# 32-column matmul tiles, and batch 2's softmax sums by way of DRAM, in a fused attention and feed-forward kernel

## The chip, the cores and the metric

The kernel runs on one core of one Trainium2 chip. The metric is the device time of one execution in microseconds. Eleven runs of the kernel before on one chip lie within 0.2 % (506.83 to 507.83 us). All comparisons here are between runs in the fast state of the chip. The rounds ran on several chips, on which the kernel before took 507.07 to 507.42 us in the median; so differences between runs of different rounds are good to some 0.3 us, and the ratios to the kernel before are the safer measure.

## The reference

Eight batches of eight heads go through an attention whose keys and values are first projected from 1024 positions to 64; its result goes through a feed-forward layer.

```python
k_proj = einsum('ks,bhsd->bhkd', E, k)          # q, k, v: 8 x 8 x 1024 x 64; E, F: 64 x 1024
v_proj = einsum('ks,bhsd->bhkd', F, v)
scores = q @ k_proj.transpose(0, 1, 3, 2) / 8
attn = exp(scores - max); attn = attn / (sum(attn) + 1e-9)
x = (attn @ v_proj), heads side by side         # 8192 x 512
h = x @ w_in                                    # 512 x 2048
g = h * clip(h + 3, 0, 6) / 6
out = g @ w_out                                 # 2048 x 512
```

## The kernel before

TensorE (PE) works nearly all the time (busy 99 % of the span), mostly on the feed-forward layer. Between groups of its matmuls the kernel makes short *visits* to the attention of later batches. One batch takes about 60 us: 2 blocks of 512 tokens, each with 16 groups of `w_in` (4 matmul rounds each) and 4 groups of `w_out` (16 rounds each). So a batch has 8 *stages* of four `w_in` groups and one `w_out` group, and a visit is hung on a stage.

Every stationary operand of 128 columns is split in two, so that two matmuls work side by side on the array (in the chain of waits 256 of them take 27.75 us, 128 rounds of 0.216 us):

```python
    width = [P // 2]
    def in_columns(ps, stationary, moving, **flags):
        for lo in range(0, stationary.shape[-1], width[0]):
            nc.tensor.matmul(ps[lo:lo + width[0]], stationary[:, lo:lo + width[0]], moving, **flags)
```

Projecting a batch frees its raw k and v and starts a chain: the projected keys are transposed by DMA, mostly the queries too, and only when that has landed does GpSimd issue the next batch's loads (for batch 4 it sat idle 35.23 us until the keys had landed, and issued the first load at 139.58 us). The two projections share one bank. The sums of exponentials are found on PE, and from batch 3 on they take a detour: logarithm and exponential give reciprocals in a few rows, which are stored in DRAM and read back once for each head, spread over 64 partitions.

```python
        def project(self, alloc):
            ps = self.ps = alloc()
            for so in range(SO):
                for e in range(2):
                    in_columns(ps[e * KP:(e + 1) * KP], ef_t[e][:, so, :], kqv[self.b]["kv"[e]][:, :, so, :],
                               start=(so == 0), stop=(so == SO - 1))
        def turn(self):
            nc.sync.dma_start_transpose(self.kT, self.kp.rearrange("p h a d -> p (h a d)"))
            last = self.kT[:1, 0, :1]
            if self.b not in (2, 3):
                qT_dma[self.b] = q_transposed(self.b)
                last = qT_dma[self.b][:1, 0, 0, :1]
            if self.b + 1 < B:
                mark = att.tile([1, 1], bf16, tag="mark", name="mark")
                nc.gpsimd.tensor_copy(mark, last)
                load_kqv(self.b + 1, "kvq" if self.b in (1, 3) else "qkv")
        # ...
        def all_sums(self, alloc):                 # batches 3 to 7: 32-column tiles, two banks
            tiles = [alloc() for _ in range(2)]
            for h in range(H):
                j, a, c = h // 2, h % 2, h % 4
                nc.tensor.matmul(tiles[h // 4][32 * c:32 * c + 32].rearrange("p (r n) -> p r n", r=2),
                                 halves.rearrange("p t i -> p (t i)"), self.aT[j][:, :, a, :],
                                 start=True, stop=True)
            return tiles
        def spread(self, den):
            few = att.tile([P, 2, TOK], f32, tag="few", name="few", bufs=1)
            inverse(few, den)
            rows = dram.tile([H, NB, TOK], f32, tag="rows", name="rows")
            nc.sync.dma_start(out=rows.rearrange("(k c) t n -> (c t) k n", k=2), in_=few[::16])
            self.recs = [rec_tile() for _ in range(KO)]
            for h in range(H):
                nc.sync.dma_start(out=..., in_=rows[h:h + 1]...to_broadcast([D, NB * TOK]))
```

Here `b` is the batch in the feed-forward layer, `second` is batch b+1 and `third` batch b+2; `n` is the stage. Batch 2 (at b = 1) has four visits of its own with its sums on PE. From b = 3 on the plan is: scores of three of the four pairs of heads, with the projection of the batch after next right behind them, then sums with the first values, products, and the last values.

```python
                if (b, n) == (2, 3):
                    return lambda: third.projected(pmm), nothing
                if n == 0:
                    return nothing, lambda: second.some_scores(
                        (1, 2, 3), ((pmm, pmm), (pat, pat), (pat, pmm)), third)
                if n == 2:
                    return second.sums_and_values, nothing
                if n == 5:
                    return second.first_products, nothing
                if n == 6:
                    return lambda: second.last_values(third), nothing
```

The softmax here doesn't subtract the row's maximum and nothing guards it: scores larger than these inputs give would overflow.

## Time and profile before

| | before |
|---|---|
| time, median of three runs | 507.55 us (507.52 to 507.98) |
| span of the profiled run | 505.5 us |
| PE busy | 498.9 us (99 %), 4858 matmuls |
| VectorE, ScalarE busy | 48 %, 51 % |
| instruction queue | 38 packets, 0.62 MB |

In the page, a line such as `PE 498.9 (99%) x4858` is an engine's busy time, its share of the span and its instructions. In a timeline, a row is a start, a duration, an engine, a source line, the operation and its tiles; at its end, in brackets, stand the idle time of the engine before it and what ended that. The chain of waits is the series of pieces that ended last, back from the end. The idle time in brackets runs from the end that the profile gives the last matmul. Counted from start to start, less one round of 0.216 us, the same wait is some 0.2 us longer; the expectations mostly count so (2.45 us where the brackets have 2.29). What these views say of this kernel is in the prediction.

### The profile page before, as it was taken

To read this page: it belongs to the slowest core of one execution; us is meant where nothing else is said; L and a number is where in the kernel's file an instruction comes from. 1 tells how busy PE (TensorE), PEld (TensorE's weight loads), DVE (VectorE), ACT (ScalarE), POOL (GpSimd) and SP (SyncE) were. 2 spreads that over 40 slices of the span, in tenths; PEclk is the share of its full clock that TensorE was granted. 3 is DMA by queue.
4 is the path that set the end of the run, shared out by engine and by line. 5 is a ranking of instruction groups with operands and counts; after the bars stand their busy time and mean duration, and the time that the engine had idled before them with its cause. 6 is when DMAs were issued, how large, how long until landed. Compare 5 with 4: busy or idle time off the path is not lost.

```text
span 505.5 us, 11242 instructions
## 1 busy us (share of the span) xinstructions
PE 498.9 (99%) x4858; PEld 259.5 (51%) x4858; DVE 245.1 (48%) x384; ACT 256.1 (51%) x438; POOL 38.7 (8%) x58
## 2 busy tenths in 40 slices
PE   8999999999999999999999999999999999999997
PEld 4554554554454555545554555545555555555554
DVE  3572736865733564536635455533752446334420
ACT  3757466566565444653555544654455544344431
POOL 8620020020020020020001000000000000000000
PEclk9999999999999999999999999999999999999999
DMA  9999979799299999699416992248110361101112
GB/s 168 198 205 208 200 131 231 142 155 202 73 151 194 230 169 190 137 154 249 123 43 118 205 249 69 61 100 209 43 43 29 82 164 43 39 26 43 43 43 84
DMA packets 78074, 66.30 MB, mean 131 GB/s; under 512 B 36216, under 2 KB 67192, under 8 KB 78024
## 3 DMA queue, kind: packets, MB, share of 16 engines
q0 software_dynamic: 32480, 29.36, 37.4%
q1 hardware_dynamic: 45320, 35.89, 27.7%
q8 instruction: 38, 0.62, 0.5%
q10 hardware_dynamic: 224, 0.33, 0.2%
q14 instruction: 12, 0.10, 0.1%
HBM read 69.73 MB, written 16.94 MB: 171 GB/s over the span
## 4 chain that ended last, share of the span: by engine, by line
PE 85%; DMA 12%; POOL 2%; ACT 1%; issue 0%; DVE 0%; ACTq 0%; POOLq 0%
PE mm L172 79%; DMA q<-in_q_dram 6%; DMA w_in_sb<-in_moe_w_in_dram 2%; PE at L172 2%; DMA v<-in_v_dram 2%; DMA qT<-q 2%; PE at L251 1%; PE at L233 1%; PE mm L251 1%; POOL q L106 1%; PE mm L271 1%; POOL k L110 1%; ACT aT L242 0%; PE mm L233 0%; POOL v L110 0%
## 5 line engine op out<-in xcount | busy, mean ns | idle before, releaser
L512 DVE SCALAR_TENSOR_TENSOR g<-r,mm 128x512 bf16<-128x512 f32 x256 | 173.5, 686 | 178.7 <-ACT r L511 177.9
L172 PE MATMUL mm<-w_out_sb,g 128*64 128x512 bf16 (+2 forms) x2080 | 235.0, 376 | 0.2 <-DVE g L512 0.2
L172 PE MATMUL mm<-xT,w_in_sb 128*64 128x512 bf16 x2048 | 231.5, 379 | 0.3
L511 ACT ACTIVATE r<-mm 128x512 f32<-128x512 f32 x256 | 152.2, 599 | 74.5 <-PE mm L172 73.5
L172 PEld LDWEIGHTS <-w_in_sb 128*64 128x64 bf16 x2048 | 117.2, 110 | 104.0 <-issue 0.8
L172 PEld LDWEIGHTS <-g 128*64 128x64 bf16 x2080 | 116.2, 110 | 105.5 <-issue 7.0
L546 ACT COPY o_sb<-mm 128x512 f32<-128x512 f32 x55 | 32.2, 586 | 126.7 <-PE mm L172 126.7
L264 DVE TENSOR_TENSOR xT<-at,rec 128x512 bf16<-128x512 f32 x42 | 26.5, 681 | 6.5 <-ACT rec L184 6.5
L242 ACT ACTIVATE aT<-at 128x512 bf16<-128x512 f32 x38 | 20.2, 615 | 9.1 <-PE at L233 9.1
L208 DVE CAST kp<-at 64x512 bf16<-64x512 f32 x12 | 7.7, 677 | 15.9 <-PE at L172 15.9
L223 POOL COPY mark<-qT 1x1 bf16<-1x1 bf16 x4 | 0.7, 176 | 165.0 <-DMA qT<-q 165.0
L242 ACT ACTIVATE aT<-mm 128x512 bf16<-128x512 f32 x18 | 10.3, 613 | 3.9 <-PE mm L233 3.9
L546 DVE COPY o_sb<-mm 128x512 f32<-128x512 f32 x8 | 5.5, 687 | 13.8 <-PE mm L172 13.8
L172 PE MATMUL at<-v,f_t 128*64 128x512 bf16 x48 | 11.4, 381 | 0.3 <-DMA v<-in_v_dram 0.3
L172 PE MATMUL at<-k,e_t 128*64 128x512 bf16 x48 | 11.6, 382 | 0.0
L264 DVE TENSOR_TENSOR xT<-mm,rec 128x512 bf16<-128x512 f32 x14 | 9.0, 685 | 4.3 <-PE mm L251 4.3
L184 ACT ACTIVATE rec<-rec 128x1024 f32<-128x1024 f32 x10 | 10.6, 1060 | 0.3
L178 ACT ACTIVATE rec<-mm 128x512 f32<-128x512 f32 x10 | 5.5, 595 | 7.9 <-PE mm L251 5.4
L178 ACT ACTIVATE few<-mm 128x512 f32<-128x512 f32 x10 | 5.4, 594 | 7.4 <-PE mm L271 7.4
L93 PE MATMUL mm<-ones 128*128 128x512 bf16 x18 | 7.4, 549 | 1.5 <-DVE halves L84 1.5
L172 PEld LDWEIGHTS <-e_t 128*64 128x64 bf16 x56 | 5.7, 110 | 6.0 <-issue 1.8
L211 DVE CAST vp<-at 64x512 bf16<-64x512 f32 x12 | 8.3, 694 | 0.4
(73 smaller groups left out, 155.0 us busy)
## 6 DMA issues: line engine op xcount, KB each, us to landing
out_dram<-o_sb SPq DMA_DIRECT2D x63, 256.0 KB, 3.0
rec<-rows SPq DMA_DIRECT2D x40, 256.0 KB, 6.5
k<-in_k_dram POOLq DMA_DIRECT2D x7, 1024.0 KB, 15.0
v<-in_v_dram POOLq DMA_DIRECT2D x7, 1024.0 KB, 20.7
q<-in_q_dram POOLq DMA_DIRECT2D x7, 1024.0 KB, 10.0
w_out_sb<-in_moe_w_out_dram POOLq DMA_DIRECT2D x4, 512.0 KB, 16.0
w_in_sb<-in_moe_w_in_dram POOLq DMA_DIRECT2D x5, 256.0 KB, 9.7
k<-in_k_dram POOLq DMA_DIRECT2D x4, 256.0 KB, 5.5
```

Of the source, the lines that this page charges most:

```text
L93: nc.tensor.matmul(ps, ones[:, :P], ones, start=True, stop=True)
L172: nc.tensor.matmul(ps[lo:lo + width[0]], stationary[:, lo:lo + width[0]], moving, **flags)
L178: nc.scalar.activation(rec[:, i], den, AF.Ln)
L184: nc.scalar.activation(flat, flat, AF.Exp, scale=-1.0)
L208: nc.vector.tensor_copy(self.kp[:, :, a, :], self.ps[:KP].rearrange("p (h d) -> p h d", d=D))
L211: nc.vector.tensor_copy(self.vp[a * KP:(a + 1) * KP], self.ps[KP:].rearrange("p (h d) -> p h d", d=D))
L242: nc.scalar.activation(self.aT[j][:, r].rearrange("p a n -> p (a n)"), tiles[r], AF.Exp, scale=scale)
L251: nc.tensor.matmul(tiles[t][c:c + D].rearrange("p (r n) -> p r n", r=2), stationary(r, 2 * j + a), self.aT[j][r:r + KP, :, a, :], start=Tr ...
L264: nc.vector.tensor_mul(self.xT[:, j, t, :], av[t], rec[:, t])
L511: nc.scalar.activation(r, h_ps, AF.Relu, bias=0.5, scale=1.0 / 6.0)
L512: nc.vector.scalar_tensor_tensor(g[:, fo, :], r, 1.0, h_ps, op0=ALU.min, op1=ALU.mult)
L546: (copy or nc.scalar.copy)(o_sb, o_ps)
```

## The change

Its intent is to take away the remaining time in which PE changes between tile shapes (0.10 to 0.12 us a change in the trace of before), and to have fewer visits. From batch 1 on all matmuls of the stream get 32-column tiles, four side by side. The sums, which already had 32 columns, then need no change of shape; they accumulate in one bank and are separate from scores and values. Batch 2's sums also go by way of DRAM, with its scores in one visit; batch 3's scores are in one visit. Projections get stages of their own, and their order shifts by a stage or more.

```diff
-                load_kqv(self.b + 1, "kvq" if self.b in (1, 3) else "qkv")
+                load_kqv(self.b + 1, "qkv" if self.b == 2 else "kvq")
@@ sums and their spreading
+        def all_sums(self):
+            den = pmm()
+            for i in range(2):
+                for c in range(4):
+                    j, a = 2 * i + c // 2, c % 2
+                    nc.tensor.matmul(den[32 * c:32 * c + 32].rearrange("p (r n) -> p r n", r=2),
+                                     halves[:, i].rearrange("p i t n -> p (i t n)"), self.aT[j][:, :, a, :],
+                                     start=(i == 0), stop=(i == 1))
+            few = att.tile([P, TOK], f32, tag="few", name="few", bufs=1)
+            nc.scalar.activation(few, den, AF.Ln)
+            later.append(lambda: self.spread(few))
@@ the stream, from batch 1
+    width[0] = P // 4
     second = Attention(2)
     for b in range(1, B):
@@ the plan: stage: (quarter of the w_out group, what)
+        if b == 1:
+            plan = {4: (4, second.all_scores), 5: (3, second.all_sums), 6: (2, second.first_values),
+                    7: (2, lambda: second.some_values((2, 3), ((pmm, pmm), (pmm, pat))))}
+        elif b + 1 < B:
+            plan = {3: (2, third.projected) if third else None,
+                    4: (2, lambda: second.some_values((0, 1), two)),
+                    6: (2, lambda: second.some_values((2, 3), two, third))}
+            if b == 2:
+                plan.update({0: (2, second.projected), 1: (4, second.all_scores), 2: (4, second.all_sums),
+                             5: plan.pop(4)})
+            else:
+                plan.update({0: (4, lambda: second.some_scores((1, 2, 3), ((pmm, pmm), (pat, pat), (pat, pmm)))),
+                             1: (4, second.all_sums)})
-            if b == 1 and t == 1:
-                qT_dma[3] = q_transposed(3)
+        if b == 1:
+            later.append(lambda: qT_dma.update({3: q_transposed(3)}))
... (cut: halves gets an extra axis; values and scaling split; batch 1's projection two groups later)
```

More of the change, by code (lines that the diff above doesn't have):

```diff
@@ L82 @@
     nc.vector.memset(ones, 1.0)
-    halves = consts.tile([P, NB, KP // 4], bf16, name="halves")
+    halves = consts.tile([P, 2, 2, NB, KP // 8], bf16, name="halves")
     nc.vector.memset(halves, 0.0)
-    for t in range(NB):
-        nc.vector.memset(halves[t * KP:(t + 1) * KP, t, :], 1.0)
+    for i in range(2):
+        for t in range(NB):
+            nc.vector.memset(halves[t * KP:(t + 1) * KP, i, i, t, :], 1.0)
     ident = consts.tile([P, P], bf16, name="ident")
@@ L237, in scores, with exps @@
             return tiles
-        def exps(self, j, tiles):
-            self.aT[j] = att.tile([P, 2, 2, HT], bf16, tag="aT", name="aT", bufs=KO + 1)
+        def exps(self, j, tiles, when=lambda f: f()):
+            self.aT[j] = aT = att.tile([P, 2, 2, HT], bf16, tag="aT", name="aT", bufs=KO + 1)
             for r in range(2):
-                nc.scalar.activation(self.aT[j][:, r].rearrange("p a n -> p (a n)"), tiles[r],
-                                     AF.Exp, scale=scale)
+                when(lambda r=r: nc.scalar.activation(aT[:, r].rearrange("p a n -> p (a n)"), tiles[r],
+                                                      AF.Exp, scale=scale))
         def quads(self, stationary, j, allocs):
@@ L260, in values, with scaled, spread @@
             return self.quads(lambda r, h: self.vp[r:r + KP, h, :], j, allocs)
-        def scaled(self, j, av, rec):
+        def scaled(self, j, av, rec, when=lambda f: f()):
             for t in range(NB):
-                nc.vector.tensor_mul(self.xT[:, j, t, :], av[t], rec[:, t])
-        def all_sums(self, alloc):
-            tiles = [alloc() for _ in range(2)]
-            for h in range(H):
-                j, a, c = h // 2, h % 2, h % 4
-                nc.tensor.matmul(tiles[h // 4][32 * c:32 * c + 32].rearrange("p (r n) -> p r n", r=2),
-                                 halves.rearrange("p t i -> p (t i)"), self.aT[j][:, :, a, :],
-                                 start=True, stop=True)
-            return tiles
-        def spread(self, den):
-            few = att.tile([P, 2, TOK], f32, tag="few", name="few", bufs=1)
-            inverse(few, den)
-            rows = dram.tile([H, NB, TOK], f32, tag="rows", name="rows")
-            nc.sync.dma_start(out=rows.rearrange("(k c) t n -> (c t) k n", k=2), in_=few[::16])
+                when(lambda t=t: nc.vector.tensor_mul(self.xT[:, j, t, :], av[t], rec[:, t]))
+        def all_sums(self):
+            den = pmm()
+            for i in range(2):
+                for c in range(4):
[6 more added lines that the diff above has]
+            later.append(lambda: self.spread(few))
+        def spread(self, few):
+            nc.scalar.activation(few, few, AF.Exp, scale=-1.0)
+            rows = dram.tile([H * NB, TOK], f32, tag="rows", name="rows")
+            nc.sync.dma_start(out=rows, in_=few[::8])
+            by_head = rows.rearrange("(c i t) n -> i c (t n)", c=4, t=NB)
             self.recs = [rec_tile() for _ in range(KO)]
@@ L284, in spread, with projected, all_scores, some_scores @@
                 nc.sync.dma_start(out=self.recs[h // 2][h % 2 * D:(h % 2 + 1) * D].rearrange("d t n -> d (t n)"),
-                                  in_=rows[h:h + 1].rearrange("h t n -> h (t n)").to_broadcast([D, NB * TOK]))
-        def projected(self, alloc=pat):
-            self.project(alloc)
+                                  in_=by_head[h // 4, h % 4:h % 4 + 1].to_broadcast([D, NB * TOK]))
+        def projected(self):
+            self.project(pat)
             self.keys_out()
-            rest = [lambda: self.values_out(0), lambda: None, lambda: None, lambda: self.values_out(1)]
-            if alloc == pmm:
-                for r in rest:
-                    r()
-                rest = []
-            later.extend([self.turn] + rest)
-        def some_scores(self, js, allocs, following=None):
-            tiles = [self.scores(j, *alloc) for j, alloc in zip(js, allocs)]
+            later.extend([self.turn, lambda: self.values_out(0), lambda: None,
+                          lambda: self.values_out(1)])
+        def all_scores(self):
+            tiles = [self.scores(j, *two) for j, two in enumerate(((pmm, pmm), (pat, pat), (pat, pat), (pmm, pmm)))]
+            for j in (0, 3, 1, 2):
+                self.exps(j, tiles[j], later.append if j in (1, 2) else lambda f: f())
+        def some_scores(self, js, allocs):
+            tiles = [self.scores(j, *two) for j, two in zip(js, allocs)]
             for j, two in zip(js, tiles):
                 self.exps(j, two)
-            if following:
-                following.projected()
-        def sums_and_values(self):
-            den = self.all_sums(pmm)
+        def first_values(self):
             self.av = [self.values(j, pat, pat) for j in range(2)]
-            self.spread(den)
         def first_products(self):
@@ L314, in first_products, with some_values, visit @@
                 self.scaled(j, self.av[j], self.recs[j])
-        def last_values(self, following):
-            av = [self.values(2, pmm, pmm), self.values(3, pat, pat)]
+        def some_values(self, js, allocs, following=None):
+            av = [self.values(j, *two) for j, two in zip(js, allocs)]
             if following:
                 following.some_scores((0,), ((pat, pat),))
-            for i in range(2):
-                self.scaled(2 + i, av[i], self.recs[2 + i])
-        def visit(self, n, following):
+            for j, two in zip(js, av):
+                self.scaled(j, two, self.recs[j])
+        def visit(self, n):
             if n == 0:
-                self.some_scores((2, 0, 1), ((pmm, pmm), (pat, pat), (pat, pat)))
+                js = 2, 0, 1
+                tiles = [self.scores(j, *two) for j, two in zip(js, ((pmm, pmm), (pat, pat), (pat, pat)))]
+                for j, two in zip(js, tiles):
+                    self.exps(j, two)
                 return lambda: None
@@ L348, in visit @@
             self.scaled(2, early, self.rec)
-            if following:
-                following.project(pat)
-                later.extend([following.turn] + [lambda a=a: following.values_out(a) for a in range(2)])
-            def rest():
-                self.scaled(3, av, rec)
-                if following:
-                    following.keys_out()
-            return rest
+            return lambda: self.scaled(3, av, rec)
     class First:
@@ L614 @@
         pop()
-        if fo == 7:
+        if fo == 9:
             second.projected()
@@ L622 @@
             pop()
-            if i == 0:
-                rest.append(second.visit(c, None))
+            if i == (c == 0):
+                rest.append(second.visit(c))
             elif i == 2 or c == SB - 1:
@@ L637 @@
         third = Attention(b + 2) if b + 2 < B else None
-        def visits(b, n):
-            def nothing():
-                pass
-            if b == 1:
-                n -= SB
-                if n < 3:
-                    return lambda: second.visit(n, third), nothing
-                return nothing, lambda: second.visit(n, third)()
-            if b + 1 < B:
-                six = (pmm, pmm), (pat, pat), (pat, pat)
-                if (b, n) == (2, 0):
-                    return lambda: second.some_scores((2, 0, 1), six), nothing
-                if (b, n) == (2, 1):
-                    return lambda: second.some_scores((3,), six[1:2]), nothing
-                if (b, n) == (2, 3):
-                    return lambda: third.projected(pmm), nothing
-                if n == 0:
-                    return nothing, lambda: second.some_scores(
-                        (1, 2, 3), ((pmm, pmm), (pat, pat), (pat, pmm)), third)
-                if n == 2:
-                    return second.sums_and_values, nothing
-                if n == 5:
-                    return second.first_products, nothing
-                if n == 6:
-                    return lambda: second.last_values(third), nothing
-            return nothing, nothing
+        plan = {}
+        two = (pmm, pmm), (pat, pat)
+        if b == 1:
[11 more added lines that the diff above has]
+                             1: (4, second.all_sums)})
         for t in range(NB):
-            if b == 1 and t == 1:
-                qT_dma[3] = q_transposed(3)
             g = g_tile()
@@ L683 @@
                     continue
-                inside, after = visits(b, t * SB + fo // SB)
-                rows = second_group(*behind[0], fo // SB, nc.vector.tensor_copy if b == 1 else None)
-                next(rows)
-                next(rows)
-                rest = inside()
-                whole(rows)
-                after()
-                if rest:
-                    rest()
+                n = t * SB + fo // SB
+                if (b, n) == (1, 7):
+                    second.first_products()
+                when, act = plan.get(n) or (None, None)
+                rows = second_group(*behind[0], fo // SB,
+                                    nc.vector.tensor_copy if second and act == second.all_scores else None)
+                for quarter in range(1, SB + 1):
+                    next(rows) if quarter < SB else whole(rows)
+                    if quarter == when:
+                        act()
             behind = [(b, t, g)]
+        if b == 1:
+            later.append(lambda: qT_dma.update({3: q_transposed(3)}))
         second, xT = third, x_next
```

## The prediction

> **What bounds the kernel now.** I read the page first: engine totals, then the shares of the chain that ended last.
>
> ```profile
> span 505.5 us, 11242 instructions
> ...
> PE 498.9 (99%) x4858; PEld 259.5 (51%) x4858; DVE 245.1 (48%) x384; ACT 256.1 (51%) x438; POOL 38.7 (8%) x58
> ...
> PE 85%; DMA 12%; POOL 2%; ACT 1%; issue 0%; DVE 0%; ACTq 0%; POOLq 0%
> ```
>
> The tensor engine carries the chain; the DMA share is the start. A busy PE need not be at its rate, so I counted starts in the timeline around one visit of the attention inside the feed-forward stream (the second batch ahead: values, then scores).
>
> ```profile
> 243.23 1.89 PE L172 MATMUL mm<-w_out_sb,g 128*64 128x512 bf16 x16
> 245.06 0.41 PE L251 MATMUL mm<-aT,vp 64*64 64x512 bf16 x4
> 245.30 0.39 PE L251 MATMUL at<-aT,vp 64*64 64x512 bf16 x4
> 245.51 0.39 PE L233 MATMUL at<-qT,kT 64*64 64x256 bf16 x8
> 245.83 1.92 PE L172 MATMUL mm<-w_out_sb,g 128*64 128x512 bf16 x16
> ```
>
> Matmuls go in rounds, one on each tile of the array at once: two 64-column ones in the stream, four 64x64 ones in a visit. The chain of waits has 256 of L172 in 27.75 us, so 128 rounds of 0.216 us. Sixteen of L172 (8 rounds, 1.73 us) take 243.23 to 245.06, 1.83: 0.10 is lost on the way in. The visit lasts 0.77 for two rounds of 512 columns (0.43) and two of 256 (0.22): 0.12 is lost on the way out. **A visit costs 0.22 us beyond its work.** The visit with the sums has a third change, from 32-column to 64x64 tiles:
>
> ```profile
> 214.82 1.46 PE L172 MATMUL mm<-w_out_sb,g 128*64 128x512 bf16 x12
> 216.21 0.61 PE L271 MATMUL mm<-aT,halves 128*32 128x512 bf16 x8
> 216.75 0.63 PE L251 MATMUL at<-aT,vp 64*64 64x512 bf16 x8
> 217.31 1.92 PE L172 MATMUL mm<-w_out_sb,g 128*64 128x512 bf16 x16
> ```
>
> Two rounds of sums (0.43) take 216.21 to 216.75, 0.54: the third change is 0.11. After 89 us I find PE waiting in two places only. One is 139 to 140 us (0.30, scores of batch 3 behind a bank). The other is this, in the last batch with a successor; the chain of waits shows it beside the batch before:
>
> ```profile
> 305.90 15.66 PE mm L172 x144
> ...
> 322.34 1.85 PE at L172 x16
> 324.19 12.09 PE mm L172 x112
> 336.27 0.55 PE mm L271 x8
> ...
> 365.89 15.68 PE mm L172 x144
> ...
> 384.47 0.66 ACT aT L242
> 385.13 0.50 ACT r L511
> ...
> 385.65 0.70 DVE g L512
> ...
> 386.39 8.82 PE mm L172 x80
> 395.22 0.55 PE mm L271 x8
> ```
>
> Six exponentials stand in ScalarE's queue before the next relu, and three of the four feed-forward banks are theirs. In the batch at 305.90 the projection of a later batch (the 16 matmuls at 322.34) keeps PE at work meanwhile; at 365.89 there is none. 305.90 to 336.27 is 30.37, less the projection (8 rounds, 1.73) 28.64; 365.89 to 395.22 is 29.33. **Without the projection behind them, these exponentials cost 0.69 us.**
>
> [...] The instruction queue's 0.62 MB in 38 packets agrees; how it keeps pace at twice the density no run here shows.
>
> **The change part by part.**
> *32-column tiles.* From batch 1 each 64-column matmul becomes two of 32; PE's listing grows from 9718 to 17126 rows. A round becomes four instead of two, for the same columns, so it stays 0.216. Evidence: four tiles at once in scores run 16 matmuls in 0.44 us, 0.11 a round of 256 columns, with a weight load each. I count 0 for the rate. [...]
> *Sums without a change of mode.* They now have the stream's tiles. Batches 3 to 7 lose one change each: 5 x 0.11 = 0.6.
> *Batch 2.* Before: four visits of 0.77 or 0.78 in the chain plus 0.10 in front of each, 3.5. After: scores 8 rounds of 0.11 (0.87), sums 2 of 0.216 (they were 4), values 4 (0.87), three visits of 0.22: 2.8. Saves 0.7.
> *Batch 3.* Scores in one visit instead of two: 0.22. The 0.30 wait at 139 goes, since the scores come a stage later than the projection: 0.5 in all.
> *Batch 1.* The projection waits 0.5 us for v at 54.7, its scores 0.3 for the transposed queries at 68.8. Both move later by two groups and a quarter, but so do the keys, and the transpose queues behind them on the same queue: I count 0.3.
> Savings: 0.2 + 0.6 + 0.7 + 0.5 + 0.3 = 2.3.
> *Projections apart.* In batches at b = 3, 4, 5 the projection leaves its place behind the six exponentials: 3 x 0.69 = 2.1 lost. (b = 6 pays already.)
> *Scores in one visit* take all eight banks. The last needs the output's bank, whose copy on VectorE ends about 0.42 + 0.69 + 0.05 = 1.16 us after the last output matmul starts; the matmul is due at 0.31 + 0.13 + 5 x 0.11 = 0.99. Twice 0.17: 0.35.
> *End of batch 2's values.* Four first products stand on VectorE just ahead of four last ones (0.6 each, from row starts at 131.9 and 132.5), and the next batch's first matmul needs a bank and an input from them. Eight at 0.6 from 1.65 us into the stage put the fifth at 4.75; PE is there at about 4.5. 0.3 lost.
> *Batch 2's sums via DRAM.* In batch 3 the sums ran at 154.5, the first row of recs was issued at 160.5, and they landed 3.7 to 6.8 us later: 11 us for the first pair of heads, 17 for all. Now about 13.5 us lie between sums and first product (0.9 + 7.5 + 3.5 + 1.65). A slack of 2 us, while batch 3's inputs still load: I book 0.3.
> *Batch 3's projection later* starts the loads of batch 4 at about 144 instead of 139.6; v took 15.2 from issue, so it lands near 160 and is wanted near 161. I book 0.2.
> Losses: 2.1 + 0.35 + 0.3 + 0.3 + 0.2 = 3.2. Net +0.9: 508.5. Two items are chances and the bank waits may overlap a little, so I take 508.3.
>
> **The rivals.** *PE's instruction supply becomes the bound.* Eight instructions per 0.216 us is 27 ns each; the trace shows such density only in bursts of a few tens[...]. [...] For it: nothing shown sustained. Against it: bursts at half that spacing. 5%.
> *The exponentials cost nothing new*, because the wait seen once was special to the last batch: then the savings win, about 506. Against it: same banks, same order, same engine in the new text.
> *A DMA comes late* (recs of batch 2, or v of batch 4): one stall of 2 to 4 us, 510 to 512. For it: landings of v spread from 7 to 29 us over the kernel.
> *A round gets shorter* with four tiles: 1 ns is 1.8 us. The four-tile rounds of 256 columns show no sign.
>
> **Range and chances.** Savings are good to 0.5, the three exponential waits to 0.7, DMA to +3. 505.5 to 511.5 holds eight in ten. Faster by over 2% needs 10 us, which no part has: 0.02. Slower by 2% needs the instruction supply or several late transfers: 0.06.
>
> **What would show it.** Right: 0.216 between rounds of four in the stream; sums of batches 3 to 7 in 0.43 with no gap before them; three waits of 0.6 to 0.7 on relu and g after the scores at b = 3, 4, 5; PE idle at 139 gone. Wrong: gaps spread evenly over L175 or "issue" waits (supply); PE or VectorE released by a rec or v landing near 120 to 165 us; no wait after the exponentials.

## The result

| | before | after |
|---|---|---|
| time, median of six runs each | 507.42 us (507.09 to 507.98) | 513.36 us (511.95 to 515.05) |
| ratio of the fast runs | | 1.0122 [1.0099, 1.0144] |
| span, clock of the profiled run | 505.5 us, 1.000 | 513.1 us, 0.995 |

A ratio is the mean time of one kernel's fast runs over that of the other's of the same rounds, so it is not quite the ratio of the medians beside it. The change loses 5.9 us. That is within 2 %, as predicted, but the time lies 1.9 us above the range. The profiled run of after was one of the slower ones, 514.99 us.

The page of the changed kernel, engine totals and the shares of the chain:

```profile
PE 500.3 (97%) x8562; PEld 253.6 (49%) x8562; DVE 244.8 (48%) x384; ACT 242.5 (47%) x425; POOL 38.7 (8%) x58
...
PE 84%; DMA 8%; ACT 3%; POOL 2%; issue 1%; DVE 1%; SPq 1%; POOLq 0%; DVEq 0%; ACTq 0%
```

PE's share of the span fell from 99 to 97 %; ScalarE's share of the chain rose from 1 to 3 %. The chain of waits in the middle of the kernel (start, duration, what, count) shows why, and what worked:

```profile
270.10 0.65 ACT aT L245
...
271.28 0.70 DVE g L511
...
275.66 0.43 PE mm L275 x8
276.09 12.09 PE mm L175 x224
```

The last two lines are good news. The sums (L275) take two rounds in 0.43 us with no loss ahead of them. The next 224 matmuls are 56 rounds of four in 12.09 us, 0.216 a round; before, 112 matmuls in rounds of two took the same 12.09. So width costs PE no rate here. The lines above them are the predicted loss: exponentials of scores (aT) and the products behind them (g) stand in the chain, for PE waits on them. This comes four times, near 210, 271, 331 and 392 us; before it came only in the last place.

Two waits on DMA are new. The timeline of PE in the changed kernel has these two rows in the second and third batch (only the rows with a wait):

```profile
133.15 1.05 PE L175 MATMUL mm<-xT,w_in_sb 128*32 128x512 bf16 x16 [2.00 <-DVE xT L267]
...
165.21 0.39 PE L175 MATMUL at<-v,f_t 128*32 128x512 bf16 x2 [2.29 <-DMA v<-in_v_dram]
```

The first is released by VectorE's products of batch 2 (by the fifth of eight, which starts at 132.40), and VectorE's own timeline says what held these up:

```profile
130.27 1.29 DVE L267 TENSOR_TENSOR xT<-at,rec 128x512 bf16<-128x512 f32 x2 [0.83 <-DMA rec<-rows]
132.40 1.99 DVE L267 TENSOR_TENSOR xT<-mm,rec 128x512 bf16<-128x512 f32 x3 [0.84 <-DMA rec<-rows]
```

The reciprocals read back from DRAM came last: the first landed at 125.67 us, the sixth, which the fifth product needs, at 132.28, and the eighth at 133.62, 1.1 us apart on average. The second wait is for v of batch 4. Its load was issued at 148.62 us (before: 140.45) and landed at 165.17, while the projection came up at 162.54, at the same time as before (162.52, where it found its data). Right after this wait the table by stretch of time (columns: length, then busy time and count of each engine, the granted clock, DMA share, GB/s) shows a second loss:

```profile
166.00:168.00 2.00, 2.00 (x32) 0.98 (x24) 0.29 (x1) 0.00 (x0) 0.00 (x0) 0.60 1.23 229
168.00:170.00 2.00, 2.00 (x28) 0.93 (x24) 0.99 (x2) 0.00 (x0) 0.00 (x0) 0.54 1.10 291
```

The clock (0.60 and 0.54 of full speed over two stretches of 2 us) was halved for some 3.4 us: rounds took 427 ns, the missing 0.40 and 0.46 of 2 us are 1.7 us lost, and the half clock lasted twice as long. The idle time ahead of it was 2.29 us (2.45 from start to start). What sets off such a stretch this one trace does not show; the experiments have longer waits to set beside it.

Finally, the instruction queue of the changed kernel (packets, MB, share of 16 engines' time):

```profile
q8 instruction: 67, 1.10, 0.9%
```

That is 67 packets of 16 KB for 38.

### The profile page after: what moved, and what is told of

It is laid out like the page before. It is cut to its first block, busy times and chain, and to the rows that moved or that the text cites. A ratio compares the mean times of both kernels' runs of the same rounds, so it can differ in the third digit from the quotient of the medians.

```text
span 513.1 us, 18654 instructions
## 1 busy us (share of the span) xinstructions
PE 500.3 (97%) x8562; PEld 253.6 (49%) x8562; DVE 244.8 (48%) x384; ACT 242.5 (47%) x425; POOL 38.7 (8%) x58
## 4 chain that ended last, share of the span: by engine, by line
PE 84%; DMA 8%; ACT 3%; POOL 2%; issue 1%; DVE 1%; SPq 1%; POOLq 0%; DVEq 0%; ACTq 0%
PE mm L175 78%; DMA v<-in_v_dram 5%; PE at L175 2%; ACT aT L245 2%; DMA rec<-rows 1%; PE mm L254 1%; DMA rows<-few 1%; DMA kT<-kp 1%; PE at L254 1%; POOL q L109 1%; SPq L290 1%; DVE g L511 1%; POOL k L113 1%; ACT o_sb L545 0%; ACT r L510 0%
## 5 line engine op out<-in xcount | busy, mean ns | idle before, releaser
L175 PE MATMUL mm<-w_out_sb,g 128*32 128x512 bf16 (+3 forms) x3904 | 237.4, 377 | 0.7 <-DVE g L511 0.7
L175 PE MATMUL mm<-xT,w_in_sb 128*32 128x512 bf16 (+1 forms) x3840 | 232.6, 379 | 2.6 <-DVE xT L267 2.0
L175 PEld LDWEIGHTS <-g 128*32 128x32 bf16 (+1 forms) x3904 | 113.9, 98 | 110.7 <-issue 9.6
L175 PEld LDWEIGHTS <-w_in_sb 128*32 128x32 bf16 (+1 forms) x3840 | 113.1, 98 | 110.8 <-issue 5.9
L267 DVE TENSOR_TENSOR xT<-at,rec 128x512 bf16<-128x512 f32 x31 | 19.9, 683 | 6.6 <-ACT rec L187 5.8
L267 DVE TENSOR_TENSOR xT<-mm,rec 128x512 bf16<-128x512 f32 x25 | 16.2, 687 | 6.6 <-PE mm L254 5.7
L175 PE MATMUL at<-v,f_t 128*32 128x512 bf16 (+1 forms) x104 | 13.8, 391 | 2.3 <-DMA v<-in_v_dram 2.3
L175 PE MATMUL at<-k,e_t 128*32 128x512 bf16 (+1 forms) x104 | 13.8, 387 | 0.0
L175 PEld LDWEIGHTS <-e_t 128*32 128x32 bf16 (+1 forms) x104 | 6.0, 98 | 4.9
L535 DVE COPY o_sb<-mm 128x384 f32<-128x384 f32 x1 | 0.6, 557 | 15.2 <-PE mm L175 15.2
L175 PEld LDWEIGHTS <-f_t 128*32 128x32 bf16 (+1 forms) x104 | 5.9, 99 | 3.4 <-issue 3.0
## 6 DMA issues: line engine op xcount, KB each, us to landing
w_out_sb<-in_moe_w_out_dram POOLq DMA_DIRECT2D x4, 512.0 KB, 15.9
```

Source lines behind the costliest of these rows:

```text
L267: when(lambda t=t: nc.vector.tensor_mul(self.xT[:, j, t, :], av[t], rec[:, t]))
```

## The experiments

Sixteen runs were made, of fifteen kernels, all with correct results; so the four groups of sums side by side in one bank came out right in every kernel that has them, v_later among them. Below, "before" is the kernel before in the same rounds on the same chip.

### The two waits for DMA

**v_later**: batch 4's projection a stage later, so that its v has landed.

```diff
-                             5: plan.pop(4)})
+                             5: plan.pop(4), 4: plan.pop(3)})
```

> The changed kernel with the projection of batch 4 one stage (6.9 us) later; nothing else moves. In the changed kernel's trace PE stood 2.45 us in front of v of batch 4, which landed at 165.2. Theory: that wait goes in full, and with it the stretch of half clock after it (up to 1.8 us in the runs that had it): 2.4 to 4.2 us faster than the changed kernel, about 510. Rival (the wait is shadowed: the time comes back at a later wait, for instance the scores of batch 4 on its late queries): less than 1 us.

Measured: 511.14 us (510.45 to 511.30), before 507.36, ratio 1.007 [1.0058, 1.0082]. That is 2.2 us less than after in the medians and 2.6 by the ratios, at the lower end of the 2.4 to 4.2 expected. The wait at 162 us is gone and the others stay.

**busy_wait**: the same wait, but ten matmuls of ones ahead of it keep PE active.

```diff
         def projected(self):
+            if self.b == 4:
+                busy(10)
             self.project(pat)
```

> The changed kernel with ten dummy matmuls (2.2 us, results unused) in front of the projection of batch 4, where PE waits 2.45 us for v. Theory: PE idles no more than some 0.3 us there, so the granted clock stays at 1.0 between 165 and 171 us; the time is that of the changed kernel's runs without a slow stretch, or up to 0.3 more: 512 to 513, with less spread. Rival (the clock fell for another reason): a stretch of half clock remains near 166 in some runs, and the time is 0.2 to 0.3 above the changed kernel's.

Measured: 513.19 us (512.79 to 514.13), before 507.36, ratio 1.0116 [1.0101, 1.013]. The median stayed, the slowest run is 0.9 us below the slowest of after, and the trace has no half-clock stretch behind the wait (granted clock 1.00 from 162 to 172 us, where after had 0.60 and 0.54). In these two traces, then, the half clock came with PE's idle time. It is not in all runs of after, whose spread of 3 us and clocks of 0.995 to 1.000 may be just this; the unchanged median says that it is no part of the typical loss.

**recs_bf16**: v_later, with the reciprocals sent in half the bytes.

```diff
-            nc.scalar.activation(few, few, AF.Exp, scale=-1.0)
-            rows = dram.tile([H * NB, TOK], f32, tag="rows", name="rows")
-            nc.sync.dma_start(out=rows, in_=few[::8])
+            half = att.tile([P, TOK], bf16, tag="half", name="half", bufs=1)
+            nc.scalar.activation(half, few, AF.Exp, scale=-1.0)
+            rows = dram.tile([H * NB, TOK], bf16, tag="rows", name="rows")
+            nc.sync.dma_start(out=rows, in_=half[::8])
```

> The changed kernel with the projection of batch 4 a stage later (511.14 us), and the reciprocal sums of all batches sent through DRAM in bf16 instead of f32, so half the bytes. In that kernel the eight copies of batch 2 land 1.1 us apart, and VectorE's products and then PE stand behind them, 2.4 us in all. Theory (lateness of these copies is the cost): the last copy lands some 4 us earlier, PE waits 0.3 us or less there, 509.0 or a little under. Rival (the products stand in line on VectorE anyway, whatever the copies do): less than 1 us gained, over 510.

Measured: 508.61 us (508.24 to 508.74), before 507.07, ratio 1.0027 [1.0015, 1.004]: 2.5 us less than v_later in the medians, 2.2 by the ratios. The last reciprocals landed at 131.34 us, not 133.86, and PE's wait near 131 us shrank from 2.4 to 0.33 us, counted from start to start. The four pairs of waits behind the exponentials stay.

### The exponentials

**proj_back**: after, with the projections of batches 5 to 7 put back behind the six exponentials.

```diff
-                plan.update({0: (4, lambda: second.some_scores((1, 2, 3), ...)),
-                             1: (4, second.all_sums)})
+                plan.pop(3)
+                def scores_then_projection():
+                    second.some_scores((1, 2, 3), ...)
+                    if third:
+                        third.projected()
+                plan.update({0: (4, scores_then_projection), 1: (4, second.all_sums)})
```

> The changed kernel with the projection put back behind the six exponentials in the blocks b = 3, 4, 5 (as in the kernel before); batches 2 and 3 as changed. Theory: three of the four pairs of waits of 0.32 and 0.33 us go, 1.9 us faster than the changed kernel, about 511.4, and only the last block keeps its pair. Rival (the waits cost nothing because something later would wait instead, such as a landing of v): within 0.5 us of the changed kernel.

Measured: 511.39 us (510.63 to 514.10), before 507.36, ratio 1.009 [1.007, 1.0109]: 2.0 us less than after in the medians, 1.6 by the ratios. In the trace of after a pair of these waits costs 0.65 us, counted from start to start, so three make 1.95. Only the last of the four pairs is left. The two waits for DMA are still there.

### The width

**w32_alone**: the kernel before, with only the width changed.

```diff
+    width[0] = P // 4
     second = Attention(2)
```

> The kernel before with one line added: tiles of 32 columns from batch 1 on; its sums now need no change of tiling when PE comes from the stream. Theory (tile width does not set the rate; the loss is in two late transfers and in the exponentials): a round stays 0.216 us, five changes of mode of 0.11[...] fall away, so 0.5 to 0.9 us faster than before, 506.5 to 507.0. Rival (twice the instructions cost the time, as issue gaps or contention): slower than before by up to the whole 6 us, 508 to 513, and gaps in the stream.

Measured: 510.05 us (508.58 to 512.43), before 507.36, ratio 1.0062 [1.0041, 1.0083]. This was a miss: a gain of 0.6 had been expected, and it is a loss of 2.7. The rounds are unchanged, and each of the five stages with sums saves 0.12 us. But the timeline of PE now has a wait for v of batch 5:

```profile
204.65 0.39 PE L172 MATMUL at<-v,f_t 128*32 128x512 bf16 x2 [1.58 <-DMA v<-in_v_dram]
```

In the kernel before this v landed at 201.53 us, 0.8 us ahead of its use. Now the loads were issued 3.5 us later and v landed at 204.61.

**w32_v5**: the same, with batch 5's v loaded ahead of its q.

```diff
-                load_kqv(self.b + 1, "kvq" if self.b in (1, 3) else "qkv")
+                load_kqv(self.b + 1, "kvq" if self.b in (1, 3, 4) else "qkv")
```

> The kernel before with 32-column tiles alone ran at 510.05 us; in its trace every stage with sums is 0.12 us shorter, as expected, but PE waits 1.75 us for v of batch 5, whose load was issued 3.5 us later than in the kernel before. This kernel is the same with the loads of batch 5 in the order k, v, q instead of q, k, v, so v lands some 5 us earlier. Theory (width costs nothing in PE, only a slack of 0.8 us was used up): 506.6 to 507.0, 0.4 to 0.8 below the kernel before. Rival (the narrower tiles lose time in other places too, that the one trace did not show): 508.5 or more.

Measured: 507.71 us (506.85 to 508.32), before 507.07, ratio 1.0009 [0.9996, 1.0021]. The wait is gone, but 0.7 us more than the upper end of what was expected is left. About 0.8 us turned up at the very end of the kernel (below).

**after_w64**: after, with 64-column tiles.

```diff
-    width[0] = P // 4
+    width[0] = P // 2
```

> The changed kernel with 64-column tiles, all else as changed. Theory (the waits for the copies and for v are those of the new order, not of the tiles): 1.2 us slower than the changed kernel, 513.5 to 515, with the waits of 2 to 3 us near 131 and 163 us still there. Rival (the denser instruction stream makes the transfers late): the waits shrink by 1 us or more each, 511 to 512.5.

Measured: 512.05 us in the median of the four fast runs (511.82 to 512.61), before 507.24, ratio 1.0096 [1.0083, 1.0109]. So 64 columns are 1.3 us faster in this order, though each stage with sums changes the tile shape again. The fifth run, 579.83 us, was the profiled one and slow, at a clock of 0.852, so its trace compares with nothing. Hence the same kernel once more, **after_w64_again**, for a trace only:

> The changed kernel with 64-column tiles once more, for a trace in the fast state. If the narrow tiles made the DMA waits longer, the wait at 131 us for the reciprocals is shorter than the 2.2 us lost with 32 columns, and so is the wait at 163 us for v of batch 4 (2.45 us). If both are as long, the width acts elsewhere.

Measured: 511.88 us in its one run, clock 0.999; its state is unknown for want of others, but the time is that of the fast runs of after_w64. The timeline of PE (rows with a wait):

```profile
131.79 1.49 PE L175 MATMUL mm<-xT,w_in_sb 128*64 128x512 bf16 x12 [0.60 <-DVE xT L267]
...
164.01 0.38 PE L175 MATMUL at<-v,f_t 128*64 128x512 bf16 x1 [1.46 <-DMA v<-in_v_dram]
```

With one more wait of 0.57 at 133.84, the reciprocals cost 1.17 us here and 2.00 with 32 columns; v costs 1.46 and 2.29. So in these two traces both waits are 0.83 us longer with the narrow tiles. Two traces are little, and other 32-column traces with the same order of work up to there can be looked at. The wait for the reciprocals is 2.10 us in v_later, 2.51 in proj_back and 2.47 in busy_wait, longer than 1.17 in each. The wait for v is 1.38 in proj_back, no longer than with 64 columns. From the start of batch 3's projection to the landing of v it is 26.8 us in after, 25.9 in proj_back and 26.2 here. So in these traces the first wait is 0.83 us or more longer with the narrow tiles; for the second no such growth is shown.

**zero_adds**: before, with a matmul of a single column of zeros behind each 64-column matmul that does not close its sum. It has nearly as many instructions as with 32-column tiles, but hardly more columns go through the array. Only its transfers were to be read.

```diff
             nc.tensor.matmul(ps[lo:lo + width[0]], stationary[:, lo:lo + width[0]], moving, **flags)
+            if nought and not flags["stop"]:
+                nc.tensor.matmul(ps[lo:lo + width[0], :1], stationary[:, lo:lo + width[0]], nought[0],
+                                 start=False, stop=False)
```

> The kernel before, with a matmul of one column of zeros that adds nothing after each 64-column matmul of batches 1 to 7 that doesn't close its sum: about as many matmul instructions as with 32-column tiles, but hardly more columns streamed through the array. Only the transfers are to be read from it, not its time, which must grow. Theory that the doubled instruction stream is what slows the transfers: the transpose of batch 3's queries, issued among the loads of batch 3, lands some 18 us after its issue as in the 32-column runs, and the load of batch 4's q ends later than 19.6 us after its issue. Rival, the doubled reading of the moving tile: it lands after about 16 us as in the 64-column runs.

Measured: 555.96 us in two runs, 62 instruction packets. Inconclusive for what it was made for: the landing of the transpose is not in its trace. Its issue took 15.10 us, as against 13.55 to 13.85 in the three 64-column kernels and 13.9 to 16.2 in the five 32-column kernels that have the same transpose among the loads; but batch 4's q landed 19.55 us after its issue, just as before (19.59). It serves below for the end of the kernel.

### Putting the gains together

**best** kept only what had seemed to gain: 32 columns, the sums in one bank, batch 3's scores in one visit, a later start of batch 1's projection. Batch 2's sums are on PE as before, and projections stand behind exponentials. **best_w64** is the same with 64 columns.

```diff
-            plan = {4: (4, second.all_scores), 5: (3, second.all_sums), ...}
+            plan = {SB + i: (2, lambda i=i: rest.append(second.visit(i))) for i in range(3)}
+            plan[7] = (4, fourth)          # last visit of batch 2, then batch 3's projection
```

> The parts of the change that the traces call gains, without those that they call losses: 32-column tiles, sums in one bank without a change of mode, batch 3's scores in one visit, the later start of batch 1; but batch 2's sums by matmul as before, batch 3 projected at the end of block 1 as before, and the other projections behind the exponentials as before. Theory: 507.4 less 0.7 (width, sums), 0.3 (batch 3) and 0.3 (batch 1): 505.9 to 506.5, faster than both. Rival (the denser instruction stream delays loads whatever the plan): 507 or more, with waits for k, v or q in the trace.

> As the run of the gains alone, with 64-column tiles. Theory: the change of mode at the sums of five batches comes back, 0.6 to 0.7 us slower than with 32 columns: 506.6 to 507.2. Rival (narrow tiles lose time through late loads): as fast as with 32 columns, or faster, and with less spread.

Measured: 506.66 us (506.08 to 507.84) and 506.78 us (506.59 to 507.38), before 507.07, ratio 0.9995 for both, [0.9981, 1.0009] and [0.9983, 1.0008]. No gain to be told from none, and none of the width, although the traces have 0.21 us less at each of five stages with sums for 32 columns.

**repaired** was best with batch 2's sums by way of DRAM too, all reciprocals in bf16, batch 3 projected at the end of block 1, and one pair of the six exponentials handed to later groups. **repaired_f32** sends the reciprocals in f32; **repaired_w64** has 64 columns.

```diff
@@ in scores_then_projection, for b = 3 to 6
+                    for i in (0, 2, 1):
+                        second.exps(1 + i, tiles[i], (lambda f: f()) if i != 1 else later.append)
@@ after each w_out group
+                if (b, n) == (1, 7):
+                    third.projected()
... (cut: tiles; the sums in bf16; the place of batch 3's query transpose)
```

> The change with every wait that the traces named repaired: batch 3's projection back at the end of block 1 (its loads go out earlier, and its 1.7 us of PE work stand in front of the products), the other projections back behind the exponentials, two of the six exponentials put off behind the next relus, and the reciprocal sums sent in bf16. Batch 2's sums stay via DRAM, tiles stay at 32 columns. Theory (these waits are the whole loss, and the change's savings are real): no wait over 0.2 us after batch 1, 505.3 to 506.2, faster than the kernel before. Rival (savings were never there): 507 or more with no wait in the trace.

> The same with the reciprocal sums in f32. Theory: the copies of batch 2 land as late as in the changed kernel, but 1.7 us of projection now stand in front of the products' users: of the wait of 2.4 us some 0.6 is left, 505.9 to 506.8. Rival (the projection waits too, since its bank comes from the first products): 2 us or more are left, over 507.5.

> The repaired kernel with 64-column tiles: the sums of six batches now cost a change of mode each way, 0.21 us by the trace of the gains alone at 64 columns. Theory: 1.2 to 1.3 us slower than the repaired kernel. Rival (the denser stream costs about as much in late transfers as it saves in mode changes): within 0.5 us of it, with less spread.

Measured: 512.67 us (511.87 to 512.99), 514.79 (512.78 to 515.02) and 510.44 (508.07 to 510.83), before 507.24. A clear miss, by my own ordering. The transpose of batch 3's queries had stayed in its old place, ahead of the reciprocals on the same queue and among the loads; it was issued at 110.58 us, took 13.90 to issue, and landed at 128.60. The rows could be sent at 126.82 only. The timeline of PE in repaired:

```profile
133.96 0.53 PE L254 MATMUL at<-aT,vp 64*64 64x512 bf16 x2 [4.85 <-DVE xT L267]
```

Still, the three show two things. Behind this one wait repaired has no other of over 0.2 us, so deferring the exponentials does remove the last pair, too. And with the transpose in the way 64 columns are 2.2 us faster: the transpose took 15.91 us from issue to landing there and 18.02 with 32 columns (16.56 and 18.53 in best_w64 and best), and the wait behind it was 3.58 us and not 4.85. The wait is not all of the difference. Behind it repaired ran at half clock, which repaired_w64 did not (1.00 throughout):

```profile
134.00:136.00 2.00, 2.00 (x18) 0.68 (x21) 1.65 (x3) 0.00 (x0) 0.00 (x0) 0.53 0.65 193
136.00:138.00 2.00, 2.00 (x28) 0.84 (x24) 1.96 (x5) 0.11 (x1) 0.00 (x0) 0.62 0.47 178
```

That is again 3.4 us at half clock, 1.7 us lost. In repaired_f32, where the wait was 6.66 us, it is 6.8 us at half clock, 3.4 us lost. So waits of 2.29 us (after), 4.85 and 6.66 us were followed by 3.4, 3.4 and 6.8 us at half clock, while one of 3.58 us in repaired_w64, and one of 2.51 in proj_back, left the clock at 1.00. The length of the wait alone does not decide it; what else does was not tested.

### Every shown wait mended

**mended** is after with v_later, recs_bf16, proj_back and the deferred pair of exponentials together; **mended_w64** has 64 columns. They were run because single repairs did not yet show that the waits are the whole loss.

> The changed kernel with every wait that its trace shows after batch 1 mended at once: batch 4's projection a stage later, the reciprocals sent in bf16, the projections of batches 5 to 7 behind the six exponentials, and the middle pair of these exponentials handed to the next groups. If the waits are the whole of the loss, it is the bf16 run (508.6) less three pairs of waits that the projection behind the exponentials took away before (1.9) less the last pair (0.65, by the delayed exponentials): 505.8 to 506.3, and its trace has no wait of over 0.35 us after batch 1. Rival: something besides the waits costs time with 32-column tiles (the two short gaps of the run with batch 5's load order changed), and it stays at 507 or more.

> The same with 64-column tiles. Theory that the width gains only the mode changes of the sums (0.2 us at each of five stages) and loses only by late transfers: where no transfer is late, 64 columns are about 1 us slower than 32, 506.5 to 507.5. Rival, from the earlier pair of runs without this path through DRAM, where the two widths took the same: within 0.3 us of each other.

Measured: mended 505.71 us (505.51 to 505.88), before 507.15, ratio 0.997 [0.9956, 0.9984]; mended_w64 505.99 us (505.84 to 506.08), ratio 0.9976 [0.9963, 0.9988]. Both are a little faster than both the kernel before and the changed one. The page of mended has

```profile
PE 496.7 (99%) x8562; PEld 246.7 (49%) x8562; DVE 245.2 (49%) x384; ACT 242.8 (48%) x425; POOL 38.7 (8%) x58
```

and behind batch 1 only one wait of PE is left, near 131 us: 0.15 us by the profile's ends of matmuls, 0.33 from start to start. So the waits account for the whole of the loss. The second expectation failed: 32 columns should have been 1 us ahead and are 0.28. The traces show where most of that goes. This is the DMA view of mended from just after its last matmul to its end:

```profile
q8 instruction: 1, 0.02, 1.9%
...
out_dram<-o_sb ACTq DMA_DIRECT2D x1, 64.0 KB, 2.6
```

and the same of mended_w64, where the list of queues ends without an instruction packet:

```profile
q10 hardware_dynamic: 144, 0.07, 7.1%
issues: line engine op xcount, KB each, median us to landing
...
out_dram<-o_sb ACTq DMA_DIRECT2D x1, 64.0 KB, 1.6
```

In mended the last 16 KB of the instruction queue q8 are fetched while the last output is being stored. (It is the queue that went from 38 packets to 67 as PE's matmuls went from 4858 to 8562.) That packet took 1.9 % of 16 engines' 3.8 us, that is 1.16 us of one engine's time, and the last store took 2.6 us to land instead of 1.6. The seventeen traces other than the slow one (before, after and fifteen of the experiments) agree without exception. In the eleven with 32 columns such a packet starts between 0.2 us before and 1.0 us after the end of the last matmul, and the last store lands 1.9 to 3.0 us after its issue (2.7 in after, 2.4 in w32_v5, 1.9 in best). In the 64-column ones the last packet starts earlier, and the store lands after 1.6. zero_adds, with 62 packets but none in this place, has 1.6. The packet records say more: in all eleven the store lands 1.5 to 1.6 us after the end of the packet. That is the time that it otherwise takes from its issue (1.6 us), so by these records it waits for the packet. In them it is where the packet falls that counts, not the width of the matmuls as such. I did not try to move the packet in a 32-column kernel.

## Why the prediction was wrong

The prediction forecast a small loss, and most of its steps stand in the traces. Two of its terms, both about transfers, were far too small.

| step of the prediction | booked | what the runs showed |
|---|---|---|
| 32-column rounds: rate "0" | 0 | right: 56 rounds in 12.09 us, with both widths |
| sums without a change of mode | -0.6 | right: 0.12 us (w32_alone) to 0.21 (best against best_w64) at each of five stages |
| projections apart | +2.1 | right: 1.6 to 2.0 (proj_back) |
| end of batch 2's values | +0.3 | right: 0.33, left in mended where the reciprocals are in time |
| batch 2's sums via DRAM, "I book 0.3" | +0.3 | **2.0 of PE's idle time**, the 0.3 above in it; sending half the bytes took 2.2 to 2.5 away |
| v of batch 4, "I book 0.2" | +0.2 | **2.3 of PE's idle time**, 2.2 to 2.6 by v_later; in some runs up to 1.7 more at half clock |
| narrow tiles and transfers | not seen | about 0.8 of the wait for the reciprocals, and about 1 us at the end |

**Batch 2's sums via DRAM.** The step that failed is the "slack of 2 us". It set the time from the sums to the first product, 13.5 us (13.8 in the trace), against the 11 us that the first pair of heads needed in batch 3. But PE waits for a later product, the fifth, as the prediction's own item on the end of the values has it, and that belongs to the third pair. Where the reciprocals are in time, the products follow each other in line; in mended the fifth starts 2.4 us after the first:

```profile
128.09 2.48 DVE L267 TENSOR_TENSOR xT<-at,rec 128x512 bf16<-128x512 f32 x4
130.49 1.88 DVE L267 TENSOR_TENSOR xT<-mm,rec 128x512 bf16<-128x512 f32 x3
```

So the third pair was wanted 15.9 us after the sums. In batch 3 its copies had landed 15.4 us after them (at 169.90 us, the sums at 154.49), and the last pair's, wanted at some 17.1, after 17, a number that stands in the same sentence. The slack was half a microsecond and less, not 2. And this chain itself was slower than in batch 3. These are the sums, the store of the rows and the copies, first in batch 3 of the kernel before, then in batch 2 of the changed kernel:

```profile
154.49 0.61 PE L271 MATMUL mm<-aT,halves 128*32 128x512 bf16 x8
157.13 0.72 SPq L281 DMA_DIRECT2D rows<-few  x1
160.50 4.96 SPq L284 DMA_DIRECT2D rec<-rows  x8
...
114.38 0.60 PE L275 MATMUL mm<-aT,halves 128*32 128x512 bf16 x8
117.91 0.53 SPq L286 DMA_DIRECT2D rows<-few  x1
122.12 4.94 SPq L290 DMA_DIRECT2D rec<-rows  x8
```

The first copy was issued 7.7 us after the sums, not 6.0: the store came 0.9 us later, since the change hands the exponential ahead of it to a later group, and it landed after 4.2 us, not some 3.4. The third pair's copies had landed only 17.9 us after the sums, 2.5 more than in batch 3. All eight, of 256 KB each, took 11.5 us from the first issue to the last landing (122.12 to 133.62 us), and 8.9 with half the bytes in recs_bf16 (122.47 to 131.34). The fifth product was due at 16.2 (13.8 and 2.4), so 1.7 us were lost here; with the 0.33 of the values' end that is PE's wait.

**v of batch 4.** The loads were to start "at about 144" and v to land near 160, a microsecond before its use. They started at 147.75, 8.2 us later than before (139.58), and the trace splits this up. Batch 3's projection began at 138.33 us, 6.4 later than before (131.98). I had allowed for the later place, but not for the wait for the reciprocals, 2.0 us, which comes just ahead of it: the first late transfer made the second one later. In recs_bf16, where the reciprocals are in time, the loads do start 1.9 us earlier, at 145.81. The transpose of the keys, whose landing lets the loads go, then took 4.05 us from issue to landing, not the 2.6 of batch 2's keys. And v took 16.55 us, not 15.2. A margin of 1 us behind three links in a row was none.

Both belong to the rival "A DMA comes late", which put one stall of 2 to 4 us at 510 to 512. It happened twice, which is where 513 comes from: 508.3 and the 3.8 us by which these two waits exceed their bookings (from start to start, 2.2 less the 0.33 of the values' end less 0.3, and 2.45 less 0.2) give 512.1, and the late end of the last store, 1.1 us by the two traces (2.7 for 1.6), gives 513.2. The measured median is 513.36. This is a sum of estimates that happens to close well; the half-clock stretch of some runs is not in it.

**The width.** Taking its rate as free was right, and its price elsewhere was not thought of. "How it keeps pace at twice the density no run here shows" was the open point, but I asked it only for PE. PE got its instructions (56 rounds in 12.09 us with both widths); the transfers paid. At the kernel's end this is shown by the packet. In the middle the narrow tiles go with slower transfers: the wait for the reciprocals is 0.8 us or more longer, and the same transpose takes 2 us longer in best and repaired (18.53 and 18.02 us) than in their 64-column twins (16.56 and 15.91). For v of batch 4 no growth is shown. In the stretch of the slow transpose (110 to 129 us) w32_alone and best have three instruction packets, before and best_w64 two. That these packets are the cause there, and not that twice the matmuls name each moving operand, stays open. zero_adds did not decide it: it has two packets in that stretch, too.

Of the other terms, the savings of fewer visits and of batch 3's order were not measured one by one. Together they must be right to about a microsecond: mended gains 1.4 us on the kernel before, though it pays the late end. The first 0.2 of the savings, for leaving a visit with narrower tiles, was my estimate, and the traces do not show it: a visit of values and scores lasts 0.77 to 0.78 us in both kernels (245.06 to 245.83 us before, 250.67 to 251.44 after, and two more in each).

## What to carry to other kernels

When a result takes a detour through DRAM and comes back in several pieces, take the slack from each piece that something waits for, not from the first alone: here it was half a microsecond for the third pair and not 2. Expect the chain ahead of it to be slower in its new place (17.9 us to the third pair's landing for 15.4), and look at which queue the first piece has to wait in (behind a transpose of 13.90 us in repaired). Before moving a projection or any step that lets loads go, follow the chain of transfers to the last use and ask for several microseconds of margin: here 1 us was no margin when the wait ahead took 2.0 us, the transpose 4.05 us for 2.6 and the load 16.55 for 15.2. And more, smaller instructions at the same rate of work were not free here: in the eleven traces where a packet of instructions fell about the end of the last matmul, the last store landed 1.9 to 3.0 us after its issue, and not 1.6. Check where a transfer on the path meets the fetch of instructions.
